# A GEGLU block on one core: where the last pair's two casts and GpSimd's last block of down sums stand in the first pass

## The chip, the core and the metric

The kernel runs on one core of a Trainium2 chip. The metric is device time of one execution, in microseconds (us). A core has five engines that run side by side, each through its own queue in order: TensorE (PE, matmuls; its weight loads are shown as PEld), VectorE (DVE), ScalarE (ACT), GpSimd (POOL) and SyncE (SP), which here issues every DMA. They wait for each other through semaphores. Matmul results land in PSUM, in 8 banks of 128 x 512 fp32; everything else lies in SBUF.

## The reference

```python
g = jnp.einsum("bsd,df->bsf", x, w_gate)     # x: 1 x 2048 x 1024, bf16
u = jnp.einsum("bsd,df->bsf", x, w_up)       # w_gate, w_up: 1024 x 3584
h = _gelu(g) * u                             # tanh form of gelu
return jnp.einsum("bsf,fd->bsd", h, w_down)  # w_down: 3584 x 1024
```

## The kernel before, in words

**Passes.** The 2048 tokens go in two passes of 1024 (two halves of 512). A pass first makes h (3584 x 1024, kept in SBUF as `hT` and `hL`), then multiplies it by w_down (`down`, line 697) and writes 1024 rows of the output.

**Products.** Every large product is done with a 2x2 scheme of seven products in place of eight, which needs sums and differences of the operands. In the up projections `t1` to `t4` and `tb` are made from x, `s1` to `s4` and `sa` from the weights. The sums `s1` to `s4` are made on POOL (line 113); `sa` is a plain cast of a weight quarter from bf16 to fp32r, made on ACT (`cast`, line 122). `sa` by `t4` is the scheme's product four: `full(..., sb["sa"], t["t4"])`.

**Units and pairs.** A unit is 256 of the 3584 features; there are 14, and each has gate and up. Units 4 to 13 go in pairs. In the first pass a pair (`pair0`, line 362) splits some products once more and keeps a part for the second pass in DRAM (`pd`). The last pair, units 12 and 13, ends in `last_of_0` (line 462): `a` is unit 12, `b` unit 13; `sa` and `sb` there are their sums, and `F`, `C`, `K`, `E` are pairs of PSUM banks. PE's order in it, with the number of matmuls: `r1` by `T1` into E (4), `r3` by `T3` into K (4), `r4` by `TB` into E (4), half of unit 13's `s1` by `T4` into K (4), `s3` by `t3` into C (8), `s4` by `tb` into K (8), `sa` by `t4` into C (8). Between them ACT copies banks to SBUF (`snap`, line 127): `p5r` out of E before the `r4` matmuls, and `p5b` out of K before the `s4` matmuls write it again. DVE adds (line 110).

**Down sums.** The down projection needs differences of w_down's quarters, three tiles `m` for each of 14 blocks j. They are made once, in the first pass, and stored to DRAM (`td`) by `store_made` (line 597). Most are made by ACT and DVE (`keep_part`, line 576). Blocks 12, 13 and 11 (`BIGS[2:]`) are made by POOL in `keep_whole` (line 590): three subtractions each. Block 11's raw rows come into two tiles `raw` (line 574, issued from the hook "made"); those of 12 and 13 into a weight tile. In `last_of_0` the hook "wholes" (line 960) asks for all three blocks, one after the other, and for the store of block 12.

**Down.** `down` goes in steps. Steps 0 to 27 multiply raw rows of w_down by h: at step `kh * 14 + j` four matmuls use half of the tile that `fetch12` (line 654) loaded as tile n = step // 2. Tiles 0 to 5 are asked for in the last pair, tile n from 6 on at step `2 * n - 8` (`need12`). `make12` (DVE, two instructions for a block) makes sums of h in steps 0 to 27; `load12` fetches `td` back (lines 612 to 623); from step 28 on the products with those follow. `more(step)` (line 1023) adds to the steps of the first pass: at 5 the store of block 13's tiles, at 9 that of block 11's, from 24 on the loads of the next pass's x.

**Order and slots.** Each engine's instructions run in the order in which the program writes them. Small tiles come from two pools with slots of 2 KB a partition: `k` (36 slots: raw rows, copies, casts, gelu's results) and `s` (13 slots: the sums `s1` to `s4`, POOL's `m` tiles, some of `make12`'s). A new tile takes the slot of an older one and waits for that tile's last writers and readers, so moving a line changes which slot each later tile gets and what it waits for. The DMA semaphores are used in turn: each DMA that SP issues waits until the one eight before it has landed.

Of the kernel before, what the change touches and what calls it, by code (L numbers as in the profile page):

```python
# [10 lines left out]
def kernel(  # L11
# [52 lines left out]
    BIGS = (1, 4, 12, 13, 11)  # L64
# [44 lines left out]
    def dve(out, a, b, op):  # L109
        nc.vector.tensor_tensor(out=out, in0=a, in1=b, op=op)  # L110
# [202 lines left out]
    def part(ps, lhs, rhs, start, stop=True):  # L313
        for i in range(2):
            for k in range(H):
                matmul(ps[i], lhs[i][:, k, :], rhs[k], start and k == 0, stop and k == H - 1)
# [145 lines left out]
    def last_of_0(a, roles, sa, sb, q, t, A, B, p5a, u2b, u2r, hooks):  # L462
        F, C, K, E = roles
        b = a + 1
        dve(F[1], F[1], p5a[1], SUB)
        part(E, q["r1"], T1, True)
        p5r = [snap(E[i], "p5", A[i]) for i in range(2)]
        part(K, q["r3"], T3, False)
        for i in range(2):
            dve(A[i], K[i], p5r[i], ADD)  # L470
        times(2 * a + 1, 0, gelu(F[0]), F[1])
        sb.make("sa")
        hooks("wholes", 0)
        part(E, q["r4"], TB, False)
        hooks("pd", b)
        part(K, [x[:, H:] for x in sb["s1"]], T4, False)
        hooks("home", b)
        for i in range(2):
            dve(B[i], E[i], u2r[i], ADD)
        hooks("pd", a)  # L480
        full(C, sb["s3"], t["t3"])
        p5b = [snap(K[i], "p5") for i in range(2)]
        full(K, sb["s4"], t["tb"])
        g, up = add(C, p5b)
        g = gelu(g)
        times(2 * b + 1, 1, g, up)
        full(C, sb["sa"], t["t4"])
        hadd(K, u2b, 2 * b, 1)
        squared(C, p5b, 2 * b + 1)
        return roles  # L490
# [99 lines left out]
    def keep_whole(j):  # L590
        ra, rb = wraw[j]
        m = made[j] = [slot([P, N], f32r, "m", True) for n in range(3)]
        pool(m[0], ra[:, N:], ra[:, :N], SUB)
        pool(m[1], rb[:, N:], m[0], SUB)
        pool(m[2], rb[:, :N], m[1], SUB)
# [89 lines left out]
    sa = {}  # L685
# [224 lines left out]
    for ip in range(NPASS):  # L910
        with tc.manual_schedule(engines={ENG.Activation}):
            if ip == 0:
                ws = {1: w, 2: ahead}
                late = lambda: add(cc, nxt["p1"])
            else:
                raw_of(0, F)()
                raw_of(1, C)()
            for u in range(1 if ip == 0 else 0, NU):
                if upgraded(u):
                    if u % 2:  # L920
                        continue
                    if u == FIRST:
                        S = {u: s, u + 1: sums_s(W(u + 1), pool)}
                    if (ip, u) == (0, FIRST):
                        fetch_wd(MID.values())
                        for n in range(4):
                            for c in range(2):
                                away[NH + n, c] = lambda n=n, c=c: staged(n, c)
                        away[NH + 4, 0] = lambda: hx

                    def hooks(what, n):
                        if what == "w":
                            if n < NU:
                                W(n)
                            if (ip, n) == (0, NU):
                                fetch_wd(BIGS[2:4])
                            if ip == 0 and n - 3 in JS:
                                fetch_wd(JS[n - 3][1:])
                            if ip == 0 and n - 2 == NH // 2 + 1:
                                send_out()  # L940
                            if ip == 0 and n - 3 == NH // 2 + 1:
                                move_on()
                            if ip and n <= LAST:
                                fetch_p5(n)
                        if what == "home" and n == LAST:
                            bring_home()
                        if what == "pd":
                            k = 0 if n % 2 else KH
                            nc.sync.dma_start(
                                out=pd[:, n - FIRST].rearrange("p i n -> p (i n)"),  # L950
                                in_=flat(xT[1][:, k : k + KH]),
                            )
                        if what == "made":
                            store_made(n)
                            if n == JS[LAST - 1][0]:
                                for m in range(6):
                                    fetch12(m)
                                    ahead12.add(m)
                                fetch_wd(BIGS[4:])
                        if what == "wholes" and n == 0:  # L960
                            for j in BIGS[2:]:
                                keep_whole(j)
                            store_made(BIGS[2])
                        if what == "fetch":
                            fetch_wd(JS[n + 2][:1])

                    roles = F, C, K, E
                    if ip == 0:
                        F, C, K, E = pair0(u, roles, S, t, JS[u], hooks)
                    else:  # L970
                        F, C, K, E = pair1(u, roles, S, t, hooks)
                    continue
                first = (ip, u) == (0, 1)

                def prepare():
                    if first:
                        pool_behind(t["t4"][-1])
                    if ip == 0 and u in (2, 3):
                        lo_part(u - 2, 3, K)
                    if u + 1 < NU:  # L980
                        nxt["s"] = make_s(W(u + 1), pool, nxt.get("s"))
                    if (ip, u) == (0, FIRST - 2):
                        fetch_wd(JS[FIRST][:1])

                def keep(part, ps):
                    if ip == 0 and u in (2, 3):
                        for n in ((0, 1), (), (2,))[part]:
                            lo_part(u - 2, n, ps)

                def aside(part):  # L990
                    if first and part < 0:
                        rest_of_0(part + 2)
                    if part == 0 and u + 2 < NU:
                        W(u + 2)
                        if ip and upgraded(u + 2):
                            fetch_p5(u + 2)
                        if (ip, u) == (0, 1):
                            load_lo()
                    if part == 0 and "t4" not in t:
                        t.make("t4")  # L1000

                def ahead_of_p4():
                    if u % 2 and u + 1 < NU:
                        raw_of(u + 1, F)()
                        nxt["c11"] = raw_of(u + 2, C)

                def behind_p4():
                    if "c11" in nxt:
                        nxt.pop("c11")()

                if u % 2 and not first:
                    E, K, C = C, E, K
                banks = (E, K, C) if u % 2 else (F, K, E)
                unit(
                    u, banks, s, t, late if first else None, prepare, aside, keep,
                    ahead_of_p4, behind_p4,
                )
                s = nxt.pop("s", None)

        last = ip == NPASS - 1  # L1020
        got, nxt = {}, {}

        def more(step):
            if last:
                return
            if step in (5, 9):
                store_made(BIGS[3 + step // 8])
            if step == 0:
                xT[:] = new_x()
            if step >= 24 and step % 2 == 0 and step // 2 - 12 < len(moves):  # L1030
                c, ko = moves[step // 2 - 12]
                transposing(xT, c, ko, (2 * (ip + 1) + c) * N)
            if step == 50:
                ws.clear()
                ws.update({n: load_w(n) for n in range(2)})
            if step == 58:
                got["s"] = make_s(ws[0], dve)
            if step == 62:
                got["t"] = make_t(xT)

        down(ip, F + E, K + C, last, more)
        F, K, C = K, C, F
        if not last:
            t, s = got["t"], got["s"]
# [29 lines left out]
```

## Time and profile before

| | us |
|---|---|
| median of 3 runs | 542.93 |
| the runs | 541.56, 542.93, 543.70 |
| the profiled execution's own time | 541.42 |
| its span on the engines | 539.6 |
| mean granted TensorE clock | 0.996 of full |
| PE busy | 531.9 (99%) |
| DVE, ACT, POOL busy | 367.6, 282.0, 271.1 (68%, 52%, 50%) |
| DMA | 107.71 MB, mean 200 GB/s |

A row of the profile's timeline gives start, duration, engine, source line, operation, output and inputs, shape and, in brackets, the engine's idle time before the row and what ended it; "x8" means eight instructions merged. The lines of most rows are those of small helpers (134 is every matmul, 110 every DVE instruction, 113 every POOL one), so rows are told apart by their tiles. The view of the waits adds up, for each engine, how long it sat idle and whose signal ended that. The chain of waits follows the last instruction back to whatever released it. The view by stretches gives, for a stretch of time, the busy time of each engine with its number of instructions, the granted clock (1.00 is full), the share of the 16 DMA engines that were busy (rounded sums can pass 1) and the bytes they moved.

### The profile page before, as it was taken

What the parts mean: (1) busy time and instruction counts of PE and PEld (TensorE: products, weight loads), DVE (VectorE), ACT (ScalarE), POOL (GpSimd) and SP (SyncE); (2) the same over time, 40 slices, a digit from 0 to 9 for tenths busy, and PEclk for the clock granted to TensorE, in tenths of its full rate; (3) what the DMA queues carried; (4) which work ended last, traced back from release to release, by engine and by line L of the source; (5) the groups of instructions that cost most, each with busy time, mean ns of one, the idle gap of its engine ahead of it and who ended that gap; (6) DMA issues with size and microseconds to landing.
All of it is one profiled execution on the core that took longest, in us unless ns stands there. A gap on an engine that the chain in (4) does not pass through costs nothing.

```text
span 539.6 us, 7564 instructions
## 1 busy us (share of the span) xinstructions
PE 531.9 (99%) x2389; PEld 378.2 (70%) x2389; DVE 367.6 (68%) x573; ACT 282.0 (52%) x508; POOL 271.1 (50%) x258
## 2 busy tenths in 40 slices
PE   9999999999999979999999999999999999999997
PEld 5568686868686754588886868677676685488885
DVE  2988768787777759747687463675765769776730
ACT  2557686968686831006264556556566561105351
POOL 1079967979797960000005959894779740000000
PEclk9999999999999989999999999999999999999999
DMA  9795218685767699999994744441744439465571
GB/s 246 161 238 174 78 65 286 196 293 196 233 235 244 227 381 394 354 254 218 243 314 150 185 117 118 116 116 48 228 122 114 117 124 376 184 214 169 165 242 49
DMA packets 118407, 107.71 MB, mean 200 GB/s; under 512 B 22112, under 2 KB 98656, under 8 KB 118368
## 3 DMA queue, kind: packets, MB, share of 16 engines
q1 hardware_dynamic: 118368, 107.24, 65.5%
q8 instruction: 19, 0.31, 0.2%
q14 instruction: 20, 0.16, 0.1%
HBM read 80.22 MB, written 20.97 MB: 188 GB/s over the span
## 4 chain that ended last, share of the span: by engine, by line
PE 94%; DMA 3%; ACT 1%; issue 0%; SPq 0%; DVE 0%; POOL 0%; POOLq 0%; DVEq 0%
PE bank L134 94%; DMA td<-m 1%; DMA raw<-in_w_down_dram 1%; DMA w<-in_w_up_dram 1%; ACT bank L583 0%; POOL m L113 0%; SPq L774 0%; DVE m L110 0%; ACT u L127 0%; ACT p L127 0%; ACT xT L127 0%; DVE sum L110 0%; ACT st L746 0%; SPq L793 0%; ACT g L202 0%
## 5 line engine op out<-in xcount | busy, mean ns | idle before, releaser
L113 POOL TENSOR_TENSOR s<-w 128x512 fp32r<-128x512 bf16 x102 | 120.3, 1198 | 146.6 <-PE bank L134 103.2
L134 PE MATMUL bank<-t,s 128*128 128x512 f32 x528 | 126.2, 392 | 0.0
L134 PEld LDWEIGHTS bank<-t,s 128*128 128x128 f32 x528 | 99.1, 188 | 21.4
L134 PE MATMUL bank<-xT,w 128*128 128x512 bf16 (+1 forms) x504 | 110.4, 376 | 0.2 <-DMA w<-in_w_up_dram 0.2
L134 PEld LDWEIGHTS <-w 128*128 128x128 bf16 x504 | 47.7, 98 | 58.6 <-issue 4.2
L202 ACT ACTIVATE g<-sum 128x512 f32<-128x512 f32 x81 | 51.5, 636 | 62.8 <-DVE sum L110 60.5
L127 ACT COPY p<-bank 128x512 f32<-128x512 f32 x98 | 55.7, 590 | 48.7 <-PE bank L134 48.7
L110 DVE TENSOR_TENSOR sum<-bank,p 128x512 f32<-128x512 f32 x54 | 37.1, 687 | 37.3 <-PE bank L134 27.2
L110 DVE TENSOR_TENSOR hT<-g,bank 128x512 bf16<-128x512 f32 x72 | 49.0, 687 | 17.1 <-ACT g L202 11.0
L134 PE MATMUL bank<-tb,s 128*128 128x512 f32 x216 | 55.6, 401 | 3.3 <-POOL m L113 3.3
L113 POOL TENSOR_TENSOR s<-w,s 128x512 fp32r<-128x512 bf16 x50 | 57.9, 1175 | 0.4
L113 POOL TENSOR_TENSOR s<-s,w 128x512 fp32r<-128x512 f32 x50 | 57.5, 1166 | 0.5
L110 DVE TENSOR_TENSOR bank<-bank,p 128x512 f32<-128x512 f32 x74 | 51.3, 695 | 6.4 <-PE bank L134 6.2
L122 ACT CAST tb<-raw 128x512 fp32r<-128x512 bf16 x28 | 17.4, 627 | 72.1 <-PE bank L134 37.0
L134 PE MATMUL bank<-t,sa 128*128 128x512 f32 x216 | 54.9, 397 | 0.0
L134 PE MATMUL bank<-q 128*128 128x512 f32 x208 | 51.7, 389 | 0.0
L134 PEld LDWEIGHTS bank<-tb,s 128*128 128x128 f32 x216 | 41.5, 193 | 12.7 <-POOL m L113 3.7
L134 PEld LDWEIGHTS bank<-t,sa 128*128 128x128 f32 x216 | 40.6, 188 | 9.1
L134 PEld LDWEIGHTS bank<-q 128*128 128x128 f32 x208 | 39.0, 188 | 8.1
L127 ACT COPY u<-bank 128x512 f32<-128x512 f32 x56 | 32.2, 597 | 13.9 <-PE bank L134 13.9
L122 ACT CAST sa<-w 128x512 fp32r<-128x512 bf16 x54 | 30.7, 617 | 4.6 <-POOL m L113 4.6
L110 DVE TENSOR_TENSOR q<-raw 128x512 fp32r<-128x512 bf16 x28 | 19.3, 688 | 19.3 <-DMA raw<-in_w_down_dram 13.5
(84 smaller groups left out, 660.7 us busy)
## 6 DMA issues: line engine op xcount, KB each, us to landing
raw<-in_w_down_dram SPq DMA_DIRECT2D x72, 256.0 KB, 4.9
w<-in_w_gate_dram SPq DMA_DIRECT2D x27, 512.0 KB, 4.5
w<-in_w_up_dram SPq DMA_DIRECT2D x27, 512.0 KB, 5.7
q<-td SPq DMA_DIRECT2D x52, 256.0 KB, 4.6
td<-m SPq DMA_DIRECT2D x11, 768.0 KB, 5.1
w<-td SPq DMA_DIRECT2D x6, 1024.0 KB, 9.6
pd<-xT SPq DMA_DIRECT2D x10, 512.0 KB, 5.7
p<-pd SPq DMA_DIRECT2D x20, 256.0 KB, 2.9
```

The costliest lines, as they stand in the source:

```text
L110: nc.vector.tensor_tensor(out=out, in0=a, in1=b, op=op)
L113: nc.gpsimd.tensor_tensor(out=out, in0=a, in1=b, op=op)
L122: nc.scalar.copy(out=t, in_=src)
L127: nc.scalar.copy(out=t, in_=ps)
L134: nc.tensor.matmul(ps, lhsT=lhs, rhs=rhs, start=start, stop=stop, skip_group_check=True)
L202: nc.scalar.activation(g, src, ACT.Gelu_apprx_tanh)
```

## The change

Two edits. The first moves unit 13's two casts (`sb.make("sa")`) from the middle of `last_of_0` to its head. The second takes block 11 out of the hook "wholes" and asks POOL for it at step 2 of the first pass's `down`; its store stays at step 9.

```diff
     def last_of_0(a, roles, sa, sb, q, t, A, B, p5a, u2b, u2r, hooks):
         F, C, K, E = roles
         b = a + 1
+        sb.make("sa")
         dve(F[1], F[1], p5a[1], SUB)
         part(E, q["r1"], T1, True)
         p5r = [snap(E[i], "p5", A[i]) for i in range(2)]
...
         times(2 * a + 1, 0, gelu(F[0]), F[1])
-        sb.make("sa")
         hooks("wholes", 0)
         part(E, q["r4"], TB, False)
...
                         if what == "wholes" and n == 0:
-                            for j in BIGS[2:]:
+                            for j in BIGS[2:4]:
                                 keep_whole(j)
                             store_made(BIGS[2])
...
         def more(step):
             if last:
                 return
+            if step == 2:
+                keep_whole(BIGS[4])
             if step in (5, 9):
                 store_made(BIGS[3 + step // 8])
```

`keep_whole` is unchanged:

```python
    def keep_whole(j):
        ra, rb = wraw[j]
        m = made[j] = [slot([P, N], f32r, "m", True) for n in range(3)]
        pool(m[0], ra[:, N:], ra[:, :N], SUB)
        pool(m[1], rb[:, N:], m[0], SUB)
        pool(m[2], rb[:, :N], m[1], SUB)
```

## The prediction

> **What bounds the kernel now.** I read the page first, then PE's waits, then the chain of waits, then the timeline around the one place that these point to. The page says that PE is the bound:
>
> ```profile
> span 539.6 us, 7564 instructions
> PE 531.9 (99%) x2389; PEld 378.2 (70%) x2389; DVE 367.6 (68%) x573; ACT 282.0 (52%) x508; POOL 271.1 (50%) x258
> ```
>
> A change gains only where PE stands still or runs slowly. PE's waits over the whole span are three:
>
> ```profile
> PE bank L134 <- POOL m L113: 3.3, 1, 3.3
> PE bank L836 <- PEq L1058: 0.8, 1, 0.8
> PE bank L134 <- DMA w<-in_w_up_dram: 0.2, 1, 0.2
> ```
>
> Two belong to the start. The third, 3.3 us in one piece, ends with POOL's `m`, a block of down sums, of which no matmul there needs anything. The chain of waits shows how PE comes to depend on it, and that nothing but PE follows:
>
> ```profile
> 184.46 4.76 DMA raw<-in_w_down_dram
> ...
> 189.28 6.17 DMA td<-m
> ...
> 195.58 0.57 POOL m L113
> ...
> 198.01 338.16 PE bank L134 x1504
> ```
>
> From 198.01 to 536.17 PE sets the end alone, so what is won at 198 arrives at the end unless something else becomes late. The timeline there:
>
> ```profile
> 189.05 2.90 PE L134 MATMUL bank<-forms,r 128*128 128x512 f32 x12
> 192.72 2.00 PE L134 MATMUL bank<-t,s 128*128 128x512 f32 x8
> 195.58 1.15 POOL L113 TENSOR_TENSOR m<-raw 128x512 fp32r<-128x512 bf16 x1 [1.88 <-DMA td<-m]
> 196.76 0.62 ACT L122 CAST sa<-w 128x512 fp32r<-128x512 bf16 x1 [4.65 <-POOL m L113]
> 197.28 1.06 ACT L127 COPY p<-bank 128x512 f32<-128x512 f32 x2
> 198.01 3.39 PE L134 MATMUL bank<-tb,s 128*128 128x512 f32 x8 [3.30 <-POOL m L113]
> 199.24 0.69 DVE L110 TENSOR_TENSOR sum<-bank,p 128x512 f32<-128x512 f32 x1 [5.49 <-POOL m L113]
> 201.23 1.98 PE L134 MATMUL bank<-t,sa 128*128 128x512 f32 x8
> ```
>
> Read it backwards. PE's `s4` by `tb` writes the banks K, which ACT's two copies `p` (`p5b`) must first have read. The copies stand in ACT's queue behind the second cast `sa`. That cast got the slot of block 11's first raw tile, so it waits until POOL's first subtraction of block 11 has read it (195.58 + 1.15 = 196.73). That subtraction itself took the slot of block 12's first `m` tile and waited for its store (189.28 + 6.17 = 195.45). The cast's data were there all along. DVE's `sum` waited for block 11 too, at 5.49 us, through a slot of the second raw tile.
>
> The last column but two of the view by stretches is the granted clock:
>
> ```profile
> 190.00:194.70 4.70, 4.70 (x21) 3.40 (x19) 3.08 (x5) 2.08 (x4) 3.54 (x4) 1.00 1.02 338
> 194.70:198.00 3.30, 0.01 (x1) 0.02 (x1) 0.00 (x0) 1.24 (x3) 2.31 (x2) 0.91 1.05 421
> 198.00:201.30 3.30, 3.29 (x9) 2.64 (x10) 1.96 (x4) 0.98 (x2) 1.16 (x1) 0.57 1.02 407
> ```
>
> The idle time costs twice: after it the clock was 0.57 for 3.3 us, and the eight matmuls at 198.01 took 3.39 us where the same eight at 184.52 took 1.98.
>
> **The change, part by part. What it removes.** Eight such matmuls start 1.81 us before the next group when nothing is wrong (184.52 to 186.33, 187.24 to 189.05). From 192.72 to 198.01 it was 5.29, so the stall costs 5.29 - 1.81 = 3.48 us. From 198.01 to 201.23 it was 3.22, so the low clock costs 1.41 us. Together 4.89 us: `down` would begin at 198.17 in place of 203.06.
>
> **Whether the stall really goes.** In the changed program, by the waits written into it, the casts' slots come from an earlier copy and from the sum of the gelu that ran at 185.86; both are free by 186.6. The second `p5b` copy has a new wait, for POOL's last `r4`, done before its block at 186.40. The `sum` waits for a POOL result of an earlier pair. What is late next, then: K's matmuls of `T4` end with the group at 191.79, near 192.9, the two copies need 1.1 us behind them, to 194.0, and PE wants K at 194.53. That leaves 0.5 us. C's first sum can start when its four `s3` matmuls are done, near 193.8, and PE wants C 1.81 us after K, at 196.34. The sum, the second addition, gelu and the product need some 2.7 us from 193.8 by their rows (0.69, 0.69, 0.63, 0.69), and only C's second bank, at 197.2, waits for all of them.
>
> **The casts at the head.** Two instructions, 1.12 us as a pair (the pair at 171.57). ACT has 1.43 us of idle time there, waiting for PE, ahead of the two `xT` copies at 190.04, which `r4` by `TB` waits for. They fit with 0.3 us over, and `r4` starts on that bank some 0.9 us behind the copies' release (four matmuls of `r3` lie between). I take 0; without that cover it is 1.12 us at most. They issue no DMA.
>
> **Block 11 at step 2.** Three POOL instructions, 1.15 + 2.40 = 3.55 us. It is not later but earlier: POOL has nothing between, its new slots are free when PE has used unit 13's `s1` and `s3` (192.9 to 194.5), and the raw rows land by 188.68 + 6.1 = 194.8. So it should run from about 194.1 to 197.7. Behind it POOL is idle until 289.27, so I take 0 for POOL. `keep_whole` issues no DMA; the store stays at step 9, and SP issues it at 204.87 whether POOL ended at 199.2 or at 197.7. SP's order is the same instruction for instruction. Block 11's tiles now lie in slots that two of `make12`'s instructions for block 5 take next, so DVE waits there for two stores, landing at 204.87 + 4.9 = 209.8 and 205.40 + 5.2 = 210.6. From its end at 204.66 - 4.89 = 199.8, DVE reaches them early, goes on at 211.3, and needs eight more blocks at 1.33 us: 222.0. Its next work, the first output subtraction, is wanted when step 27 ends (226.87 before, about 222.8 after). That hides it, by 0.8 us.
>
> **What is late next: the raw rows of w_down.** This is the term that I subtract. In `down` PE advances 0.864 us a step (203.06 to 218.61 for 18 steps):
>
> ```profile
> 203.06 15.71 PE L134 MATMUL bank<-raw,hT 128*128 128x512 bf16 x72
> 218.61 8.80 PE L134 MATMUL bank<-raw,hL 128*128 128x512 bf16 x40
> ```
>
> The loads do not move with PE. From 192 to 220 the DMA engines are busy without a break (share 1.04, 394 GB/s), and SP issues each transfer as the one eight before it lands. Tile 12 is the first of the pair issued at 209.81, behind two stretches of `td` of 1 MB each; it takes 9.9 us and lands at 219.7. PE needs it at step 24: 218.61 + 6 x 0.864 = 223.8 before, 4.1 us to spare; with 4.89 gained, 218.9, so PE waits 0.8 us. Tile 11 (208.65 + 7.7 = 216.35, wanted at 217.2) and tile 13 (210.72 + 9.7 = 220.4, wanted at 221.4) arrive in time, by 0.8 and 1.0. The first `td` tiles are there by 215.6, wanted at 223.2. After 229 the DMA traffic falls (268 GB/s in 224 to 232), and SP catches up.
>
> Does 0.8 us of idle time lower the clock? The rows have 3.30 us, after which it did, and 0.22 us at 7.55, after which it stayed at 1.00. The cost lies between 0 and 1.41 us. In the stall itself the mean clock was 0.91, so it fell only in the last 0.6 us of it (0.09 x 3.3 / 0.5), after 2.7 us; 0.8 is nearer to 0.22. I take 0.
>
> Sum: -3.48 - 1.41 + 0.8 = -4.1 us. Against the profiled execution's own 541.42 that gives 537.3; that execution was 1.5 us below the median of the runs, 542.93, so for the median I forecast **538.8 us**.
>
> Two rules of the Trainium skill can be weighed here. "TensorE: Matmul & The Clock Gate", part "The HAM clock gate", has the clock at half after an idle window of about 3.4 us and full again only after about 3.4 us of work. The row shows it sooner on both counts, low after 2.7 us of idle time and full again by 201; the rule would make the low clock worth 1.7 us and the sum 0.3 us larger, an estimate, and it agrees that 0.8 us does no harm. "DMA: Bandwidth & Descriptors", Specifications, gives a ceiling of 435 GB/s for the fabric; at that rate the 27.7 us of traffic up to tile 12 would take 25.2, it would land 2.5 us earlier, and the gain would be the full 4.89. The rows' 394 GB/s decide.
>
> **The rivals.** (A) Nothing is given back: tile 12 lands at 218.9 or earlier, for instance because a run's transfers are a little faster. Then -4.89: 538.0. For it: only 0.8 us is at stake; against it: the full DMA engines.
>
> (B) More is given back: the wait for tile 12 lowers the clock, or it lands 1.4 us later. Then -2.7: 540.2, on the border of what counts as faster. For it: a stall of unknown length in front of a clock that has already fallen once; against it: the 2.7 us that it took to fall.
>
> (C) The change does not do what it says: a cast or a `p5b` copy still waits for block 11. Block 11's third subtraction would end at 197.7 and PE start at about 198: 542.9. Against it: the slots named above.
>
> (D) Slower: the DMA stream itself slips against PE, at tile 12 and step 24. Up to 2.7 us of idle time PE gives back only the time; past that the clock falls and 1.41 more goes. If tile 12 lands at 222.4 (2.7 us later than now), the wait is 3.5 us and the gain is 4.89 - 3.5 - 1.41 = 0; every us later than 222.4 is a us slower, so 225.4 would give 545.9. For it: the engines have no share left. Against it: the same bytes in the same order, and no new wait ahead of them.
>
> **How the numbers follow.** Forecast 0.60, A 0.17, B 0.14, C 0.06, D 0.03. A measurement of this kernel can tell about 0.5% (2.7 us) from no change. The forecast and A are over that, B stands on it and I split it evenly: faster 0.60 + 0.17 + 0.07 = 0.84, same 0.07 + 0.06 = 0.13, slower 0.03. The range: the low end is the profiled execution's own time with the full 4.89, 536.5; the high end is B, 540.2, and the 0.8 us by which the highest run stood above the median: 541.0.
>
> **What would show it.** Right: no wait of PE for POOL's `m`; the `sa` casts at 188.6 in ACT's idle time; the eight `s4` matmuls about 1.81 us after the eight before them at clock 1.00; block 11 on POOL from about 194 to 198; `down` from about 198.2; one wait of PE of under 1.5 us, for a raw tile, near 219, with the clock still at 1.00. Wrong: a wait of PE between 194 and 198; PE late for tile 11 or for `td`; a clock under 1.00 after 219; the `sum` still waiting for POOL. Most of all it would be wrong if the landing times follow PE after all, one way or the other.

## The result, and the profile after

| | before | after |
|---|---|---|
| median of 6 runs | 542.34 us | 537.68 us |
| lowest to highest | 541.41 to 544.06 | 536.80 to 538.11 |
| the profiled execution's own time | 541.42 | 537.85 |
| ratio, after to before, with its 95% interval | | 0.9909 (0.9888 to 0.9929) |

The change is faster by 0.9%, 3.9 to 6.1 us. The page of the changed kernel opens:

```profile
span 536.1 us, 7543 instructions
PE 528.3 (99%) x2368; PEld 376.4 (70%) x2389; DVE 368.1 (69%) x573; ACT 282.1 (53%) x508; POOL 270.9 (51%) x258
```

(PE's 21 instructions fewer are records missing from this trace; PEld has all 2389.) PE's waits over the span:

```profile
PE bank L781 <- DMA xn<-in_x_dram: 1.2, 1, 1.2
PE bank L134 <- DMA raw<-in_w_down_dram: 0.9, 1, 0.9
PE bank L836 <- PEq L1060: 0.8, 1, 0.8
```

The wait for POOL's `m` is gone, and a wait for raw rows of w_down is new. The first and third belong to the start and scatter between executions (here 0.24 us worse than before). The timeline of PE, from the place of the old stall to the new one:

```profile
192.96 1.99 PE L134 MATMUL bank<-t,s 128*128 128x512 f32 x8
194.78 1.98 PE L134 MATMUL bank<-tb,s 128*128 128x512 f32 x8
196.60 1.97 PE L134 MATMUL bank<-t,sa 128*128 128x512 f32 x8
198.41 15.71 PE L134 MATMUL bank<-raw,hT 128*128 128x512 bf16 x70
213.97 5.34 PE L134 MATMUL bank<-raw,hL 128*128 128x512 bf16 x24
220.25 3.61 PE L134 MATMUL bank<-raw,hL 128*128 128x512 bf16 x15 [0.94 <-DMA raw<-in_w_down_dram]
```

From the `s3` group to `down` it is 198.41 - 192.96 = 5.45 us; before it was 203.06 - 192.72 = 10.34. The view by stretches shows the clock (last column but two) at full speed throughout:

```profile
190.00:194.50 4.50, 4.50 (x21) 3.71 (x20) 3.59 (x7) 2.63 (x5) 3.92 (x4) 1.00 1.02 330
194.50:198.00 3.50, 3.50 (x17) 2.88 (x17) 3.11 (x6) 1.45 (x3) 3.21 (x3) 1.00 1.05 418
198.00:201.30 3.30, 3.25 (x16) 1.51 (x16) 3.04 (x5) 0.36 (x1) 0.31 (x1) 1.00 1.02 414
```

ACT's and POOL's timelines hold the two edits: the casts stand in ACT's former idle time, the `p5b` copies wait for PE alone, and block 11 waits for nothing but its own raw rows:

```profile
188.75 1.12 ACT L122 CAST sa<-w 128x512 fp32r<-128x512 bf16 x2
189.94 1.08 ACT L127 COPY xT<-bank 128x512 f32<-128x512 f32 x2
...
192.69 1.11 ACT L127 COPY p<-bank 128x512 f32<-128x512 f32 x2 [1.18 <-PE bank L134]
```

```profile
194.63 1.17 POOL L113 TENSOR_TENSOR m<-raw 128x512 fp32r<-128x512 bf16 x1 [0.56 <-DMA raw<-in_w_down_dram]
195.89 2.43 POOL L113 TENSOR_TENSOR m<-raw,m 128x512 fp32r<-128x512 bf16 x2
```

The view of the raw tiles, cut to the one issue at 210.95 (tile 12), names who waited for it and how long it took:

```profile
who waited for it (us, times):
  PE bank L134: 0.9, 1
...
DMA to landing us min/median/max: 9.3/9.3/9.3
```

It landed at 220.25, at which PE went on.

### The profile page after: what moved, and what is told of

Read it like the earlier page. It is cut to its first block, busy times and chain, and to the rows that moved or that the text cites. A ratio compares the mean times of both kernels' runs of the same rounds, so it can differ in the third digit from the quotient of the medians.

```text
span 536.1 us, 7543 instructions
## 1 busy us (share of the span) xinstructions
PE 528.3 (99%) x2368; PEld 376.4 (70%) x2389; DVE 368.1 (69%) x573; ACT 282.1 (53%) x508; POOL 270.9 (51%) x258
## 4 chain that ended last, share of the span: by engine, by line
PE 92%; DMA 6%; SPq 1%; issue 0%; ACT 0%
PE bank L134 92%; DMA raw<-in_w_down_dram 3%; DMA hL<-w 1%; DMA td<-m 1%; DMA xn<-in_x_dram 1%; SPq L600 0%; SPq L657 0%; SPq L774 0%; ACT xT L127 0%; PE bank L781 0%; ACT st L746 0%
## 5 line engine op out<-in xcount | busy, mean ns | idle before, releaser
L134 PE MATMUL bank<-xT,w 128*128 128x512 bf16 (+1 forms) x489 | 107.8, 376 | 1.0
L134 PE MATMUL bank<-tb,s 128*128 128x512 f32 x216 | 54.2, 393 | 0.0
L134 PE MATMUL bank<-raw,hT 128*128 128x512 bf16 x140 | 31.2, 379 | 0.2
```

What stands on the lines that cost most here:

```text
L134: nc.tensor.matmul(ps, lhsT=lhs, rhs=rhs, start=start, stop=stop, skip_group_check=True)
```

## The experiments

Each set of experiments had its own runs of the kernel before beside it, so the ratios are to be compared, not the medians of different sets. Theory and rivals at the outset: the stall was a matter of slots (S) or of the cast's place in ACT's queue (Q); the wait at step 24 is a place in a full DMA queue (D) or moves with PE (P); the clock falls after a certain length of idle time (C) or after any idle time of a us or two (K).

| label | what | median us | ratio to before (95%) |
|---|---|---|---|
| e1_casts_only | first edit alone | 542.24 | 1.0008 (0.9992 to 1.0023) |
| e2_block_only | second edit alone | 538.60 | 0.9932 (0.9911 to 0.9953) |
| e3_after_raw_first | changed kernel, raw tiles ahead of `td` | 538.15 | 0.9925 (0.9904 to 0.9946) |
| e4_before_raw_first | kernel before, raw tiles ahead of `td` | 542.75 | 1.0002 (0.9990 to 1.0013) |
| e5_raw_first_sums59 | e3 and DVE's weight sums a step later | 536.06 | 0.9882 (0.9858 to 0.9905) |
| e6_sums59 | changed kernel, DVE's weight sums a step later | 537.43 | 0.9908 (0.9889 to 0.9927) |
| e7_act_extra9 | changed kernel, a stall of 1.9 us put in | 540.15 | 0.9944 (0.9921 to 0.9967) |
| e8_act_extra13 | changed kernel, a stall of 3.9 us put in | 542.39 | 1.0005 (0.9990 to 1.0021) |
| e9_block_raw_sums59 | e5 without the first edit | 536.52 | 0.9884 (0.9864 to 0.9903) |

**e1: the first edit alone.**

```diff
         b = a + 1
+        sb.make("sa")
         dve(F[1], F[1], p5a[1], SUB)
...
-        sb.make("sa")
         hooks("wholes", 0)
```

> Only the first edit: the two casts at the head of the last pair's end, block 11 still asked for in the pair. Theory S (a slot decides, not the cast): the slot of block 11's first raw tile falls to the next small tile that ACT makes, the gelu of F, which then waits for POOL's first subtraction with the two p5b copies behind it in ACT's queue. PE still waits about 3.3 us, the clock falls, the time is that of the kernel before within 0.5 us. Rival Q (taking the cast out of the queue ahead of p5b is what wins): PE does not wait near 195, the time falls by about 4 us as with both edits.

Nothing is won. In ACT's timeline the casts run early and without waiting; the next small tile, the gelu of F, now stands where the cast stood:

```profile
188.19 1.12 ACT L122 CAST sa<-w 128x512 fp32r<-128x512 bf16 x2
189.38 1.07 ACT L127 COPY xT<-bank 128x512 f32<-128x512 f32 x2
196.43 0.60 ACT L202 ACTIVATE g<-bank 128x512 f32<-128x512 f32 x1 [5.98 <-POOL m L113]
196.93 1.07 ACT L127 COPY p<-bank 128x512 f32<-128x512 f32 x2
```

PE waits for POOL as before, 3.3 us in one piece, at the same place. Q falls.

**e2: the second edit alone.**

```diff
-                            for j in BIGS[2:]:
+                            for j in BIGS[2:4]:
                                 keep_whole(j)
...
+            if step == 2:
+                keep_whole(BIGS[4])
```

> Only the second edit: block 11 asked for at step 2, the casts where they were. Theory S: no tile of ACT or DVE gets a slot that still waits for block 11; the casts run in ACT's idle time from 191.5 to 192.6, the p5b copies end near 193.8, PE does not wait there and waits about 0.9 us for raw tile 12: the time of the changed kernel within 0.5 us, 4 to 5 us under the kernel before. Rival Q: the casts in the middle still hold up p5b, PE waits near 195, and at most half of the gain appears.

The stall is gone without the casts' move. ACT's timeline, and the row of POOL with block 11's first subtraction:

```profile
190.79 0.62 ACT L202 ACTIVATE g<-bank 128x512 f32<-128x512 f32 x1
191.28 1.15 ACT L122 CAST sa<-w 128x512 fp32r<-128x512 bf16 x2
192.31 1.10 ACT L127 COPY p<-bank 128x512 f32<-128x512 f32 x2
...
193.81 1.18 POOL L113 TENSOR_TENSOR m<-raw 128x512 fp32r<-128x512 bf16 x1
```

The casts cost the copies nothing, since those wait for PE to finish with K until about the same time; PE's `s4` group starts at 194.34, 1.81 us behind the `s3` group, and tile 12 costs 0.35 us in this execution. The casts ended before POOL began block 11, so they did not wait for its raw tiles. By the program, the reason is the order of allocation (the profile does not show slots): when block 11 is asked for after the pair, its raw tiles are still in use as the cast, the gelu and the copies are given their slots, and these get others. The median (538.60) is 0.9 us above the changed kernel's, where S had said within 0.5, and its runs reach from 536.8 to 540.6; the profile is of the fastest of them and does not show why. e9 asks whether that is the casts' doing.

**e3 and e4: raw tiles 12 and 13 ahead of the second 1 MB stretch of td.**

```diff
-    AT12 = [12, 12, 15, 15, 18, 18, 20, 22, 24, 26, 28, 30, 31, 33]
+    AT12 = [12, 12, 18, 18, 18, 18, 20, 22, 24, 26, 28, 30, 31, 33]
```

> The changed kernel, with the second 1 MB stretch of td fetched three steps later, behind raw tiles 12 and 13. Theory D (the 0.9 us wait at step 24 is a place in a full DMA queue): tile 12 lands about 2.6 us earlier, near 217.6, the wait is gone, 0.9 us under the changed kernel, 5 to 6 us under the kernel before. The stretch itself lands near 221, wanted at about 224. Rival P (what PE waits for moves with PE; the DMA engines or the stretch of td are late whatever the order): a wait of 0.5 us or more appears at another tile or at step 30 and the time is that of the changed kernel.

> The kernel before with the same reordering of the loads alone. Theory D: tile 12 had 4.1 us to spare there, so nothing is won: within 0.3 us of the kernel before, PE's 3.3 us wait for POOL stays. Rival R (the order of the loads is worth something by itself, wherever PE stands): 0.9 us or more is won here too.

At step 24 D holds: tile 12 lands at 217.4 in e3, PE does not wait there, and from `down`'s start to step 28 it takes 24.0 us (198.04 to 222.04) where the changed kernel took 25.1 (198.41 to 223.52). In e4, where `down` began only at 203.55, nothing is won. But e3's time is that of the changed kernel, as P had said, though not for P's reason: PE is 1.5 us ahead at step 28 (0.4 of it since before `down`), and as much is given back 50 us later. The first matmuls of `sa` by `q4` start up to 0.60 us apart near 273, where 0.23 is usual, 1.5 us in sum. DVE's timeline in e3 shows why:

```profile
265.04 0.69 DVE L110 TENSOR_TENSOR s<-w 128x512 fp32r<-128x512 bf16 x1 [3.77 <-DMA w<-in_w_gate_dram]
268.36 0.69 DVE L110 TENSOR_TENSOR s<-w 128x512 fp32r<-128x512 bf16 x1 [2.63 <-DMA w<-in_w_up_dram]
...
272.58 1.88 DVE L110 TENSOR_TENSOR st<-bank,m 128x512 bf16<-128x512 f32 x3
```

At step 58 DVE is asked for the next pass's weight sums `s` ahead of the four output subtractions `st` that read the banks which PE's next product writes. It stands waiting for weights, and the subtractions read the banks from 272.6 to 275.1, with PE there at 273. PE's weight loads name it:

```profile
PEld bank L134 <- DVE st L110: 1.2, 3, 0.4
```

In the changed kernel's profile there is no such wait (the subtractions start at 272.01, PE's product at 274.51). In e1, too, it is there (matmuls up to 0.60 us apart near 279, PE at its old pace), so it is not a matter of the raw tiles' order. DVE's two waits for weights add up to 6.4 us in e3 and 5.7 in e1, and to 4.3 in the changed kernel and 4.8 in the kernel before, whose profiles show no such wait of PE: the loss seems to come and go with the landing of the weights.

**e5 and e6: the weight sums a step later.** e5 is e3, and e6 the changed kernel, with this:

```diff
-            if step == 58:
+            if step == 59:
                 got["s"] = make_s(ws[0], dve)
```

> The changed kernel with raw tiles 12 and 13 ahead of the second td stretch, as in the third experiment, and with the next pass's first eight weight sums on DVE asked for at step 59 in place of 58, so behind the four output subtractions that free the banks of the last product. Theory V (what the third experiment won at step 24 was given back at 273, where DVE stood waiting for weights ahead of those subtractions): no wait of PE or of its weight loads for them, the span falls to about 534.5 to 535, the time to 536 to 536.8, and the runs lie closer together than 2 us. Rival W (the loss near 273 is PE's or the DMA's own): matmul starts 0.55 to 0.60 us apart stay near 273, time 537.5 to 538.5.

> The changed kernel with the weight sums at step 59 alone. Theory V: the wait of 0.3 to 1 us for raw tile 12 stays; the median falls by 0 to 0.7 us below the changed kernel's, since there the subtractions were in time in the profiled run and late in some others, and the highest run falls by about a us. Rival W: no difference, same spread.

In e5 V holds. The subtractions come first and wait for PE alone, the sums find their weights landed:

```profile
268.76 1.89 DVE L110 TENSOR_TENSOR st<-bank,m 128x512 bf16<-128x512 f32 x3 [7.65 <-PE bank L134]
270.57 0.68 DVE L110 TENSOR_TENSOR st<-bank,p 128x512 bf16<-128x512 f32 x1
271.16 1.28 DVE L110 TENSOR_TENSOR s<-w 128x512 fp32r<-128x512 bf16 x2
```

PE's only waits in e5 are the two of the start. The runs lie within 0.9 us (535.83 to 536.71). e6 does not tell V from W: it has the wait for tile 12, 1.43 us in its profile, the changed kernel's ratio, and a highest run of 538.06 against 538.11, where V had forecast about a us less. So neither edit alone moves the time, and the two together do: e5's four runs lie below all six of e6 (537.22 to 538.06) that were made beside them. The reordered loads win their time at step 24 only when the sums no longer take it back.

**e7 and e8: a stall of chosen length at the old place.** n is 9 in e7 and 13 in e8; the casts repeat the same data into the same place.

```diff
+        for n in range(9):
+            nc.scalar.copy(out=sb["sa"][n % 2], in_=W(b)[:, n % 2, KH:, P:])
         p5b = [snap(K[i], "p5") for i in range(2)]
```

> The changed kernel with nine more casts of unit 13's same data, repeated into the same place ahead of the two p5b copies: a PE stall of known length at the same place. ACT does one in about 0.5 us, so PE should wait 1.7 to 2.2 us near 195. Theory C (the clock falls only after some 2.7 us of idle time): clock 1.00 after it, the eight s4 matmuls start to start 1.81 us, and 0.8 to 1.5 us over the changed kernel, since tile 12 is then no longer waited for. Rival K (any wait of a us or two lowers it): clock near 0.6 for 3 us, 3.2 us or more for the eight, 2.2 to 2.9 us over.

> The same with thirteen more casts: PE waits 3.7 to 4.4 us. Both theories: the clock falls, the eight s4 matmuls take 3.0 to 3.6 us start to start, 4 to 5.2 us over the changed kernel, about the kernel before. If the eight stay at 1.81 us, the low clock of the kernel before had another cause than the length of the wait.

C falls. PE in e7, and the same execution by stretches:

```profile
193.20 1.99 PE L134 MATMUL bank<-t,s 128*128 128x512 f32 x8
197.04 3.01 PE L134 MATMUL bank<-tb,s 128*128 128x512 f32 x8 [1.86 <-ACT p L127]
199.85 2.69 PE L134 MATMUL bank<-t,sa 128*128 128x512 f32 x8
```

```profile
195.00:197.00 2.00, 0.18 (x1) 0.00 (x0) 0.01 (x1) 2.00 (x5) 1.42 (x2) 1.00 1.05 408
197.00:199.00 2.00, 1.96 (x7) 1.57 (x8) 1.90 (x4) 1.02 (x2) 1.92 (x2) 0.73 1.04 424
199.00:201.00 2.00, 2.00 (x6) 1.63 (x5) 1.49 (x4) 0.63 (x1) 0.14 (x1) 0.50 1.03 422
201.00:203.00 2.00, 2.00 (x9) 1.21 (x9) 1.01 (x2) 0.60 (x1) 0.00 (x0) 0.92 1.03 387
```

The clock was still full through the wait of 1.86 us and fell about 0.9 us after PE was back at work (0.73 over 2 us is 1.08 us at half), until 201.3 (0.92 over 2 us is 0.32 at half): some 3.4 us. The two groups of eight took 202.38 - 197.04 = 5.34 us in place of 3.63, so the low clock cost 1.71. Nor is K the whole of it: the mean granted clock of e7's ten runs was 0.996 or 0.997 in seven, 540.4 us on average, and 1.000 in three, 538.2. So the same program seems to lose some 2 us to the low clock in some runs and nothing in others; how long PE waited in the nine runs without a profile is not known. In e8 (wait 3.92 us, the eight matmuls 201.98 - 198.43 = 3.55 us start to start) the clock fell in all ten runs, to a mean of 0.994 in four of them (543.5 us on average) and 0.996 or 0.997 in six (542.2). The profiled execution is one of the four. By stretches, for PE alone, first the kernel before and then e8:

```profile
197.42:200.83 3.41, 2.82 (x7) 0.50 1.03 417
```

```profile
195.00:197.22 2.22, 0.00 (x0) 1.00 1.05 422
197.22:204.05 6.83, 5.62 (x13) 0.50 1.04 404
204.05:206.00 1.95, 1.95 (x10) 1.00 1.07 402
```

The low stretch is 3.41 us long in the kernel before and twice that in e8, though PE was at work again from 198.43. It costs half of the PE time that falls into it: 2.82 / 2 = 1.41 us in the kernel before, and 5.62 / 2 = 2.8 in e8, where the two groups of eight took 2.7 us too long. In e1's profile (197.55 to 200.96) and e4's (198.12 to 201.53) it is 3.41 us long as well, and more of it falls on PE at work: it cost 1.67 and 1.66 us there, by the starts of the two groups and of `down`.

**e9: e5 without the first edit.**

> The fifth experiment without the first edit: the casts where they were, block 11 at step 2, raw tiles 12 and 13 ahead of the second td stretch, the weight sums at step 59. Theory S (the first edit does nothing by itself): with the two later losses out of the way it takes the time of the fifth experiment within 0.5 us, 536 to 536.6, no wait of PE near 195, 219 or 273. Rival Q (the casts at the head are worth something that the second experiment's scatter hid): 0.7 us or more over the fifth experiment, with a wait of PE near 195 or copies p5b that end past 194.3.

536.52 against 536.06, ratios 0.9884 and 0.9882: the same within what the intervals tell, about 1 us to each side. PE has no wait but the two of the start, and the `p5b` copies end at 193.78. S holds: of the two edits, block 11 brings the gain, and the casts bring nothing that these runs can tell.

The best version is e5: 6.0 us under the kernel before by the medians of its set (6.4 by the ratio, 0.9882), and 1.4 us under e6, which has the changed kernel's time.

## Why the prediction was right, point by point

- **What the stall cost.** Foreseen 3.48 us and 1.41 us for the low clock, 4.89 together. The two profiled executions give 10.34 - 5.45 = 4.89.
- **Why it goes.** The chain through the slot of the raw tile was read rightly, and so were the waits of the casts and of the `p5b` copies. One sign of being wrong seems to be there: the changed kernel's `sum` at 194.18 has 0.17 us of idle time put down to POOL's `m`. It is not block 11, which began at 194.63, and the same gap of 0.16 to 0.17 us is put down to PE in e3, e5 and e6. What the prediction did not ask is which edit breaks it. It went through both as one; e1 shows that the first alone hands the same slot to the gelu, e2 and e9 that the second alone is enough.
- **The casts at the head cost nothing.** They ended at 189.87, the copies behind them ran at once. Right, but nothing is gained by them either.
- **Block 11 from 194.1 to 197.7.** It ran from 194.63 to 198.32; its raw rows landed half a us later. Only DVE waited, for stores (below), and PE did not notice.
- **Tile 12 gives back 0.8 us.** The mechanism, the tile and the step are right. The wait was 0.94 us by its row, and step 24 began 1.10 us late: 198.41 + 24 x 0.864 = 219.15, against 220.25. Other executions had 0.35 (e2) and 1.43 (e6). The tile landed at 219.22 (e2), 220.25 and 220.47 (e6), against 219.7 before: the loads did not come earlier with PE. That is the premise on which most hung. (The side estimate of 25.2 us at the page's ceiling comes to 25.1; nothing hangs on it.)
- **This wait does not lower the clock.** It did not in any of the changed kernel's six runs (mean clock 0.999 or 1.000), but the reason given for it fell: the prediction took from one stall that the clock falls after 2.7 us of idle time, and in e7 it fell with 1.86, in e1 and e4 only after 3.2 and 3.3. That rival B did not come was less safe than the text made it.
- **The skill's rule on the clock.** The prediction said that the row showed full speed again sooner than the page has it. That compared from PE's restart. From the fall to the return the low stretch lasted 3.41 us in the kernel before, in e1 and in e4, 3.4 in e7, and 6.83, twice that, in e8. "TensorE: Matmul & The Clock Gate", under "What's actually happening", has a window of about 3.4 us that runs on regardless of the kernel. The runs agree with the length. The fall came 2.7 us behind the start of the wait in the kernel before, in e7 and in e8, and 3.2 and 3.3 us behind it in e1 and e4. That the place of a wait in such a window decides, and not its length alone, would fit this and e7's three and seven, but no run here shows where a window begins.
- **Nothing else is late.** True of PE in the profiled execution, but two margins were thinner than the text had them. DVE waited for two stores, 1.99 us until 206.73 and 2.22 until 210.98, with nine blocks of `make12` behind the second and not eight: it ended at 223.15, not at 222.0, and its first output subtraction was on time only because tile 12 held up PE. In e5, where nothing held PE up, that subtraction began 0.64 us after PE's step 28 (222.52 against 221.88; in the kernel before it was 0.19 ahead), and still no wait of PE followed. And the prediction did not look past 229 closely enough: a second wait, behind DVE's weight sums at step 58, lay less than 2 us away and took back what e3 won.
- **The size.** The sum was -4.1 us. The pair of profiled executions gives -3.57: -4.89, 1.10 for tile 12, 0.24 for a later start, and a remainder of -0.02. The medians give -4.7 and the ratio -4.9, and the median came out at 537.68 where 538.8 was forecast. Of this miss of 1.1 us, 0.6 is the starting point: 542.93 was the median of three runs, and six give 542.34. One term was too small for the median, the low clock: 1.41 us is one execution's price, and e1 and e4 paid some 0.25 more for the same stall. Of the 55 runs of the kernel before that were made beside the experiments, 42 had a mean clock of 0.996 or 0.997, like the profiled one (542.1 us on average), ten 0.994 or less (543.9) and three 0.999 or more (541.5). The clock does not explain all: the two runs of e4 with a mean of 1.000 took 542.8. How much of the rest is DVE's wait near 273 is open. The profile of the kernel before does not have it; e4's, the same but for the order of the loads, has 0.2 us of it, and e1's, the same but for the casts, 1.0.

## What to carry to other kernels

When an instruction waits for something that it does not use, look for the slot, not for the instruction: here moving the waiting instruction handed the slot to the next one in line, and moving the slow owner's allocation past the busy place ended it. Before counting on a gain on the critical engine, list what it will then reach earlier (transfers in a full queue, banks that another engine must free) with the time each has to spare; here 4.9 us were won and the two nearest had 4.1 and less than 2. And a stall of PE of 1.9 us or more cost its length and, in most runs, 1.4 to 2.7 us on top at half speed.

## What the hardware showed that was not expected

- The granted clock can fall after PE is back at work: in e7's profile 0.9 us behind the end of a 1.86 us wait, and by the mean clock in seven of its ten runs. Waits of 0.94 and 1.43 us (the profiles of the changed kernel and of e6) went with a mean clock of 0.999 or 1.000 in all twelve runs; a wait of 3.92 us with a lower one in all ten.
- The low stretch was 3.4 us long in four profiles (the kernel before, e1, e4, e7) and twice that, 6.83 us, in e8's, whose mean clock was 0.994. Each such length takes 0.003 off the mean, so the ten of 55 runs of the kernel before at 0.994 or less probably had two of them as well; none of them has a profile. They took 1.8 us more than the 42, on average.
